# Two halves of a weight matrix loaded from two queues at the start of a decode-attention kernel

## The chip, the cores and the metric

The kernel runs on one core of one Trainium2 chip. The metric is device time in microseconds (us) of one launch; the time given for a kernel is the median of its runs. The engines are called as in the profile: PE (TensorE matmul, with PEld for its weight loads), DVE (VectorE), ACT (ScalarE), POOL (GpSimd), SP (SyncE, which here only issues DMAs; SPq and ACTq are the queues of issuing instructions). Matrices are bf16, sums are float32.

## What is computed

Two independent problems, A and B, with the same shapes and tensors of their own; the two outputs are put side by side. Each is one decode step of attention over the last 4096 rows of a cache of 16384:

```python
def _A_ref(x, k_cache, v_cache, wq, wo):        # x [2, 1, 576], caches [2, 16, 16384, 128]
    W = min(4096, max(256, Sk // 4))            # 4096
    rep = Hq // Hkv                             # 32 query heads, 16 key heads: 2
    q = (x @ wq).reshape(B, Sq, Hq, Dh).transpose(0, 2, 1, 3)
    k = jnp.repeat(k_cache[:, :, Sk - W:, :], rep, axis=1)
    v = jnp.repeat(v_cache[:, :, Sk - W:, :], rep, axis=1)
    scores = jnp.einsum("bhqd,bhkd->bhqk", q, k) * (Dh ** -0.5)
    p = softmax(scores, axis=-1)
    o = jnp.einsum("bhqk,bhkd->bhqd", p, v)
    return o.transpose(0, 2, 1, 3).reshape(B, Sq, Hq * Dh) @ wo    # wo [4096, 576]
return jnp.concatenate([a, b], axis=-1)
```

Everything is read once: 2 x 2 x 32 MB of keys and values, 4.5 MB of wq and 4.5 MB of wo for each problem.

## The kernel before, in words

**Order by hand.** The kernel lists operations for each engine in the order in which that engine runs them (`S.add(engine, function, deps, tag)`), and turns the dependences into semaphore waits; waits that follow from others are left out. So the place of a call in the code is the place of its instructions in that engine's queue.

**Slabs.** Keys and values come in slabs of 4 MB (128 partitions x 32 KB), each for one group of heads: 8 K slabs and 8 V slabs for each problem, 16 steps in all (`ND`). They go through a ring of four buffers (`ring`, `NR` = 4) that the first 512 rows of each wq share: buffers 0 and 1 hold wq of A and of B, 2 and 3 the first two K slabs. The next slab of a buffer is issued by SP when its last reader is done (L241). The stream is Q A, Q B, K0, K1, V0, K2, V1 and so on; near the end K14, K15, V13, V14, V15, and V15 is cut in two pieces (L237). Slabs of wo are issued in between (L275), the last of them after V15 in one part of 576 KB and three small ones (L277, L262).

**The start.** wq has 576 rows: four chunks of 128 (`NFC`, in the ring slab) and 64 left over, the half rows, loaded on their own into `wqr` (L248). The half rows of A stand on even partitions and those of B on odd ones, 64 partitions each. SP issues A's half rows, A's slab (L250), x of B (L185), B's half rows, B's slab, K0 and K1; ACT's first instruction is the DMA of A's x. `x_sb` holds the four rows of x (two of A, two of B). DVE writes `x_dup` (L361), the last 64 columns of x interleaved for the two problems and zeroed by the mask `maskP` where the other problem's partitions lie. Five transposing products on PE (L355) turn x into columns, ACT copies them to `xT` with four repeats (L369): chunks 0 to 3 and chunk 4, the half rows.

**The queries.** `do_qpair` (from L396) runs four times, twice for each problem: for each chunk one weight load of `xT` and four products of 512 columns into four PSUM banks (first of each chunk L421, the others L170, a helper that reuses the loaded weights). ACT evacuates the banks (L435, L440), DVE transposes (L445), ACT keeps the result (L453). The first product of each problem waits for its slab and for both loads of half rows. The four banks alternate between two sets from one pair to the next.

**A step.** DVE transposes the K slab in four parts (L485), PE multiplies them with the queries (L510, L170), DVE takes the maximum (L520, L533), ACT the exponential (L555), DVE transposes the probabilities (L563), PE multiplies them with V (L601, V one step behind), ACT evacuates (L613), and after each pair of steps a chain of small operations ends in the product with wo (L756 and, for the last pair, L760).

**The end.** After the last K slab the remaining steps run out: V13, V14 and V15's first piece (24 products, L601); `do_redist(D_ // 2, 2)` with two idle products (L711 to L716: products of 512 columns that write a bank nobody reads); V15's second piece (8 products); `keep_on(2)`, a weight load and two more idle products (L727 to L733); then the last combination (L648), norm (L683, DVE) and projections (L760): eight products for the pair's first step and eight for its second, of which four wait for the first small load of wo, two for the second and two for the third. ACT and DVE copy the two halves of the output (L792, L793), ACT and SP store them (L801).

Of the kernel before, what the change touches and what calls it, by code (L numbers as in the profile page):

```python
# [6 lines left out]
BF16 = mybir.dt.bfloat16  # L7
# [52 lines left out]
def build_kernel(nc, probs, out, cfg=None):  # L60
# [28 lines left out]
    HH = HD // 2  # L89
    NXC = NFC + 1  # L90
    NOUT = wo0.shape[1]
# [15 lines left out]
    with es:  # L107
        sb = lambda name, shape, dt: es.enter_context(nc.sbuf_tensor(name, shape, dt))
        ring = sb("ring", [128, NR, SLABW], BF16)
        xt = sb("xt", [128, NKT, 2048], FP32)  # L110
        wqr = sb("wqr", [128, HD], BF16)
        wob = sb("wob", [128, 2, 8, NOUT], BF16)
        xT = sb("xT", [128, NXC, NPROB, 128], BF16)
        x_dup = sb("x_dup", [NPROB * Bb, DREM, NPROB], BF16)
        maskP = sb("maskP", [NPROB * Bb, NPROB], BF16)
        x_sb = sb("x_sb", [NPROB * Bb, D], BF16)
# [45 lines left out]
        wo_sem = [sem("wo%d" % r) for r in range(2)]  # L162
        x_sem = [sem("xload%d" % P) for P in range(NPROB)]
        wl_sem = [sem("wl%d" % n_) for n_ in range(len(HEADS))]
# [19 lines left out]
        def load_x(P, eng):  # L184
            return dma_op(eng, x_sem[P], 1, lambda e: e.dma_start(  # L185
                x_sb[P * Bb:(P + 1) * Bb, :], probs[P][0][:, 0, :]).then_inc(x_sem[P], 16), [], "xload%d" % P)
        x_dma = {0: load_x(0, "act")}

# [55 lines left out]
        def issue_wq(n, P):  # L244
            wqP = probs[P][3]
            r = n % NR
            deps = [reader[n - NR]] if n >= NR else []
            wq_dma[P] = dma_op("sp", wq_sem, 1, lambda e: e.dma_start(  # L248
                wqr[P::NPROB, :], wqP[NFC * 128:D, :]).then_inc(wq_sem, 16), [], "wqr%d" % P)
            slab_dma[n] = dma_op("sp", ring_sem[r], 1, lambda e: e.dma_start(  # L250
                ring[:, r, :], wqP[0:NFC * 128, :].rearrange("(p s) n -> p (s n)", s=NFC)).then_inc(ring_sem[r], 16), deps, "wq%d" % P)

            if P == 0:
                for P_ in range(1, NPROB):
                    x_dma[P_] = load_x(P_, "sp")
# [90 lines left out]
        def f_xT(e, bank):  # L346
            last = None
            bb = bank[:].bitcast(BF16)
            NB = NPROB * Bb
            for ch in range(NXC):  # L350
# [4 lines left out]
                last = e.transpose(bb[:, ch * NB:(ch + 1) * NB], src, ident_b[0:NB, 0:NB])  # L355
            return last
        issue_until(0)
        init_small()
        init["maskP"] = S.add("dve", lambda e: e.tensor_reduce(
            maskP[:], ident_b[0:NPROB * Bb, 0:NPROB * Bb].rearrange("d (p b) -> d p b", b=Bb), AX.X, ALU.max), [p_ident_b], "maskP")  # L360
        x_cd = S.add("dve", lambda e: e.tensor_tensor(  # L361
            x_dup[:], x_sb[:, NFC * 128:D].unsqueeze(2).broadcast_to([NPROB * Bb, DREM, NPROB]),
            maskP[:].unsqueeze(1).broadcast_to([NPROB * Bb, DREM, NPROB]), ALU.mult), [init["maskP"]] + list(x_dma.values()), "xdup")

        n_x, bank_x, op_xT = tb_job(f_xT, "xT", list(x_dma.values()) + [x_cd, p_ident_b])

        def f_xev(e):
            NB = NPROB * NXC
            return e.activation(  # L369
                xT[:].rearrange("c h p (a w) -> c (h p) a w", a=4)[:, :, :, 0:Bb],  # L370
                bank_x[:].bitcast(BF16)[:, 0:NB * Bb].rearrange("c (p b) -> c p b", b=Bb).unsqueeze(2).broadcast_to([128, NB, 4, Bb]),
                ACTF.Copy)
        op_xev = S.add("act", f_xev, [op_xT, p_zxT], "xev")
        tb_consumer[n_x] = op_xev

# [20 lines left out]
        def do_qpair(i):  # L396
            Gs = (2 * i, 2 * i + 1)
            P = Gs[0] // GPP
            nq = pos[("Q", P)]
            issue_until(pos[("Q", NPROB - 1)])  # L400
            banks = q_banks(i)
            order = [NFC] + list(range(NFC))
            if Gs[0] % GPP:
                order = order[::-1]
            todo_ = [(ch, b) for ch in order for b in range(4)]
            seen = {b: 0 for b in range(4)}
            prev = [q_free.get((i - 2, b)) for b in range(4)]
            ends = [max(n for n, (ch, b) in enumerate(todo_) if b // 2 == g) + 1 for g in range(2)]
            assert ends[1] == len(todo_)
            for g in range(2):  # L410
                def fn(e, part=todo_[(0, ends[0])[g]:ends[g]]):
                    last = None
                    for ch, b in part:
                        c0 = (b % 2) * HH + 512 * (Gs[b // 2] % GPP)
                        w_ = ring[:, nq % NR, ch * HD + c0:ch * HD + c0 + 512] if ch < NFC else wqr[:, c0:c0 + 512]
                        start, stop = seen[b] == 0, seen[b] == NFC
                        seen[b] += 1
                        if q_first[0] == (P, ch):
                            last = matmul_again(e, q_first[1], banks[b], w_, start, stop, False)
                        else:  # L420
                            last = q_first[1] = e.matmul(banks[b], xT[:, ch, P, :], w_, start=start, stop=stop)  # L421
                            q_first[0] = (P, ch)
                    return last
                op = S.add("pe", fn, [slab_dma[nq], op_xev] + list(wq_dma.values()) + prev, "q%d" % Gs[g])
                reader[nq] = op
                q_done[Gs[g]] = op
# [268 lines left out]
        def do_redist(G, idle=0):  # L695
# [14 lines left out]
            if idle:  # L710
                def f_idle(e):  # L711
# [13 lines left out]
        fin_ops = []  # L725

        def keep_on(n):  # L727
            def f(e):
                first = last = e.matmul(idle_out, ident_b[:, :], maskB[:, :], start=True, stop=True)
                for _ in range(n - 1):  # L730
                    last = matmul_again(e, first, idle_out, maskB[:, :], True, True)
                return last
            S.add("pe", f, [chain[(ND - 1, "exp")], init["maskB"]], "keep%d" % n)  # L733

# [3 lines left out]
        def do_proj(D_):  # L738
# [255 lines left out]
```

## Time and profile before

| quantity | value |
|---|---|
| median of 3 runs | 363.48 us (363.40 to 363.51) |
| profiled execution: device time / span of its records | 363.62 us / 362.3 us |
| PE / PEld / DVE / ACT / POOL busy | 62% / 16% / 56% / 19% / 10% of the span |
| bytes read | 153.10 MB, 423 GB/s over the span |
| first load issued / first data packet | 0.80 us / 2.15 us |
| last wo load seen landed by PE / span ends | 360.2 us / 362.3 us |

Times in the profile count from the start of the span. A line of the timeline gives start and duration in us, the engine, the line of the kernel, the operation, the tile written and the tiles read, and in brackets how long the engine had been idle and for whom it waited. The DMA share of a stretch is the mean busy share of the core's 16 DMA engines; it can pass 1.00 a little, as a packet is counted where it starts. PEclk is the TensorE clock that was granted, 1.00 being full speed.

### The profile page before, as it was taken

What the parts mean: (1) busy time and instruction counts of PE and PEld (TensorE: products, weight loads), DVE (VectorE), ACT (ScalarE), POOL (GpSimd) and SP (SyncE); (2) the same over time, 40 slices, a digit from 0 to 9 for tenths busy, and PEclk for the clock granted to TensorE, in tenths of its full rate; (3) what the DMA queues carried; (4) which work ended last, traced back from release to release, by engine and by line L of the source; (5) the groups of instructions that cost most, each with busy time, mean ns of one, the idle gap of its engine ahead of it and who ended that gap; (6) DMA issues with size and microseconds to landing.
All of it is one profiled execution on the core that took longest, in us unless ns stands there. A gap on an engine that the chain in (4) does not pass through costs nothing.

```text
span 362.3 us, 2755 instructions
## 1 busy us (share of the span) xinstructions
PE 224.9 (62%) x1325; PEld 57.4 (16%) x950; DVE 201.5 (56%) x175; ACT 68.7 (19%) x153; POOL 35.3 (10%) x55
## 2 busy tenths in 40 slices
PE   0399195474865647584774747575673738656775
PEld 0000021111221201111121112111121112211121
DVE  3013598483917467291936648092854839179831
ACT  1036402020300303020210203112020203002131
POOL 1000000004000040004000040001200040110020
PEclk9999589788796968889787889969697887969999
DMA  8999999999999999999999999999999999999996
GB/s 348 405 445 423 445 408 433 456 412 442 420 426 434 434 409 447 430 438 430 402 454 430 434 434 418 434 434 430 421 434 430 438 425 430 430 434 434 425 419 242
DMA packets 6943, 153.27 MB, mean 423 GB/s; under 512 B 778, under 2 KB 1300, under 8 KB 1428
## 3 DMA queue, kind: packets, MB, share of 16 engines
q1 hardware_dynamic: 6924, 153.10, 98.7%
q8 instruction: 9, 0.15, 0.2%
q14 instruction: 2, 0.02, 0.0%
q10 hardware_dynamic: 8, 0.00, 0.0%
HBM read 153.10 MB, written 0.00 MB: 423 GB/s over the span
## 4 chain that ended last, share of the span: by engine, by line
DMA 71%; DVE 14%; PE 13%; SPq 1%; issue 0%
DMA ring<-in_B_k_cache_dram 34%; DMA ring<-in_A_k_cache_dram 26%; DVE xt L485 13%; DMA wob<-in_B_wo_dram 8%; PE st L170 6%; DMA wqr<-in_B_wq_dram 4%; PE st L510 4%; PE st L421 1%; PE tb L170 1%; PE acc L170 1%; PE ot L170 1%; DVE nM L533 1%; PE tb L421 0%; PE tb L523 0%; SPq L237 0%
## 5 line engine op out<-in xcount | busy, mean ns | idle before, releaser
L485 DVE STREAM_TRANSPOSE xt<-ring 128x2048 f32<-128x2048 f32 x64 | 145.3, 2285 | 77.3 <-DMA ring<-in_B_k_cache_dram 40.1
L510 PE MATMUL st<-xt,zq 128*128 128x512 bf16 x256 | 115.8, 452 | 114.5 <-DVE xt L485 88.8
L170 PE MATMUL st<-xt,zq 128*128 128x512 bf16 x256 | 114.4, 447 | 0.0
L510 PEld LDWEIGHTS st<-xt,zq 128*128 128x128 bf16 x256 | 27.9, 109 | 210.0 <-DVE xt L485 104.1
L601 PE MATMUL acc<-ring,pC 128*32 128x512 bf16 x512 | 33.9, 381 | 2.6 <-DMA ring<-in_B_v_cache_dram 2.6
L538 ACT ACTIVATE nMrep<-nM 1x128 f32<-1x128 f32 x16 | 4.9, 308 | 142.9 <-DVE nM L533 142.9
L613 ACT ACTIVATE acc_sb<-acc 128x512 bf16<-128x512 f32 x16 | 9.5, 597 | 81.3 <-PE acc L601 81.3
L563 DVE STREAM_TRANSPOSE pC<-pR 128x1024 bf16<-128x1024 bf16 x16 | 19.5, 1216 | 3.6 <-ACT pR L555 2.1
L520 DVE TENSOR_REDUCE m<-st 128x1 f32<-128x1024 f32 x16 | 19.0, 1190 | 1.2 <-PE st L170 1.2
L620 POOL TENSOR_TENSOR acc_sb<-acc_sb,maskJ 128x1024 bf16<-128x1024 bf16 (+1 forms) x8 | 13.4, 1679 | 59.0 <-ACT acc_sb L613 59.0
L472 POOL TENSOR_TENSOR zq<-qk,maskA 128x128 bf16<-128x128 bf16 x16 | 6.3, 399 | 127.9 <-PE st L170 106.1
L555 ACT ACTIVATE pR<-st,bias_sb 128x1024 bf16<-128x1024 f32 x16 | 17.8, 1114 | 0.5
L445 DVE STREAM_TRANSPOSE qtr<-qrow 128x512 f32<-128x512 f32 x8 | 5.7, 712 | 20.8 <-ACT qrow L435 13.5
L387 ACT ACTIVATE st<-maskB 128x1024 f32<-128x1024 bf16 x16 | 16.5, 1032 | 1.6 <-POOL rsel L570 0.4
L756 PE MATMUL ot<-wob,Rsb 128*2 128x512 bf16 x56 | 15.7, 399 | 0.2 <-ACT Rsb L721 0.2
L601 PEld LDWEIGHTS acc<-ring,pC 128*32 128x32 bf16 x512 | 12.9, 95 | 16.1 <-DMA ring<-in_B_v_cache_dram 3.6
L570 POOL TENSOR_TENSOR rsel<-maskS,rsum 128x16 f32<-128x16 bf16 x8 | 1.7, 216 | 124.1 <-ACT pR L555 124.1
L170 PE MATMUL tb<-wob,Rsb 128*2 128x64 bf16 x56 | 11.1, 197 | 0.0
L355 PE MATMUL tb<-ident_b,x_sb 4*128 4x4 bf16 x4 | 0.3, 173 | 14.6 <-DVE x_dup L361 14.6
L775 DVE TENSOR_TENSOR o_rest<-o_rest,tb 2x64 f32<-2x64 f32 x3 | 0.6, 209 | 15.4 <-PE tb L170 15.4
L623 POOL TENSOR_TENSOR acc_sb<-acc_sb 128x512 bf16<-128x512 bf16 (+1 forms) x8 | 8.2, 1030 | 0.6
L533 DVE TENSOR_REDUCE nM<-tb 1x8 f32<-1x128 f32 x16 | 4.4, 272 | 6.2 <-PE tb L523 6.1
(88 smaller groups left out, 107.0 us busy)
## 6 DMA issues: line engine op xcount, KB each, us to landing
ring<-in_A_k_cache_dram SPq DMA_DIRECT2D x8, 4096.0 KB, 30.8
ring<-in_A_v_cache_dram SPq DMA_DIRECT2D x8, 4096.0 KB, 32.1
ring<-in_B_k_cache_dram SPq DMA_DIRECT2D x8, 4096.0 KB, 30.7
ring<-in_B_v_cache_dram SPq DMA_DIRECT2D x7, 4096.0 KB, 32.8
wob<-in_A_wo_dram SPq DMA_DIRECT2D x4, 1152.0 KB, 33.5
ring<-in_A_wq_dram SPq DMA_DIRECT2D x1, 4096.0 KB, 12.8
ring<-in_B_wq_dram SPq DMA_DIRECT2D x1, 4096.0 KB, 22.4
wob<-in_B_wo_dram SPq DMA_DIRECT2D x3, 1152.0 KB, 34.6
```

Source lines behind the costliest of these rows:

```text
L170: return e.add_instruction(mybir.InstMatmult(name=nc.get_next_instruction_name(), engine=i.engine, ins=[e.lower_ap(rhs), i.ins[1]], outs=[ ...
L387: chain[(s, "fill")] = S.add("act", lambda e: e.activation(ST[s % 2][:, :].rearrange("k (h j) -> k h j", h=2), maskB[:].unsqueeze(1).broad ...
L485: Xop[(s, u)] = S.add("dve", lambda e: e.transpose(xt[:, i % NKT, :].rearrange("k (j w) -> k j w", w=64), ring[:, n % NR, :].bitcast(FP32) ...
L510: first = last = e.matmul(bank, zq[:, p4, s % NZQ, w0:w0 + 128], mv, start=False, stop=stop, skip_group_check=True)
L520: chain[(s, "max")] = S.add("dve", lambda e: e.tensor_reduce(m1[:, 0:1], ST[s % 2][:, :], AX.X, ALU.max), d, "max%d" % s)
L555: chain[(s, "exp")] = S.add("act", lambda e: e.activation(pR[:, :], ST[s % 2][:, :], ACTF.Exp, bias=bias_sb[:, 0:1], scale=SCALE, accum_ou ...
L563: chain[(s, "pC")] = S.add("dve", lambda e: e.transpose(pC[:, s % NPT, :, :].rearrange("k j c -> k (j c)"), pR[:, :]), d, "pC%d" % s)
L601: last = e.matmul(ACC[32 * cb:32 * cb + 32, 0:512], pC[:, D_ % NPT, j0_:j0_ + 4, :].rearrange("k j c -> k (j c)"), ring[:, n % NR, j0_ * 1 ...
L613: acc_ev[D_] = S.add("act", lambda e: e.activation(acc_sb[:, D_ % 2, :], ACC[:, :], ACTF.Copy), d, "accev%d" % D_)
L620: t = S.add("pool", lambda e: e.tensor_tensor(v, v, maskJ[:].unsqueeze(1).unsqueeze(3).broadcast_to([128, l1 - l0, 4, 128]), ALU.mult), [a ...
L623: t = S.add("pool", lambda e: e.tensor_tensor(a_[:, :, 0:256], a_[:, :, 0:256], a_[:, :, 256:512], ALU.add), [t], "acca%d" % D_)
L756: first = e.matmul(OT[0:Bb, 0:NB0], l_, wob[:, pc, s_, 0:NB0], start=start and begin, stop=end, skip_group_check=True)
```

## The change

It has three parts.

- **Loads.** `wqr` gets a place for each problem, `[128, 2, 2048]`: each of the 64 half rows is cut in two, so that a problem's half rows lie on all 128 partitions with 2048 columns each. B's load is issued by ACT as its first instruction, while SP issues A's; both x loads go to SP, behind A's slab, on one semaphore.
- **x.** `x_dup` holds the last 64 columns of x twice, without a mask; the products that turn x write four repeats at once; ACT copies the four full chunks, and a new DVE product writes two chunks for the half rows, each zeroed by `maskP` on the partitions of the other half (`xT` has six chunks). A query bank uses the one of these two chunks that its columns belong to, so each bank still gets five products. The second half of a pair of queries also waits for the evacuations of the pair before.
- **Tail.** Three idle products instead of two behind the redistribution, listed as waiting for `fin_ops` also; `keep_on` and its two idle products are gone; the first half of the last projection is in two parts, three quarters at once and the last quarter behind the last norm.

```diff
-        wqr = sb("wqr", [128, HD], BF16)
+        wqr = sb("wqr", [128, NPROB, HH], BF16)
...
-        x_dma = {0: load_x(0, "act")}
+        x_dma = {}
...
-            wq_dma[P] = dma_op("sp", wq_sem, 1, lambda e: e.dma_start(
-                wqr[P::NPROB, :], wqP[NFC * 128:D, :]).then_inc(wq_sem, 16), [], "wqr%d" % P)
+            if P == 0:
+                for P_ in (1, 0):
+                    wq_dma[P_] = dma_op("act" if P_ else "sp", wq_sem, 1, lambda e, P_=P_: e.dma_start(
+                        wqr[:, P_, :], probs[P_][3][NFC * 128:D, :].rearrange("r (h n) -> r h n", h=2)).then_inc(wq_sem, 16), [], "wqr%d" % P_)
...
             if P == 0:
-                for P_ in range(1, NPROB):
+                for P_ in range(NPROB):
                     x_dma[P_] = load_x(P_, "sp")
...
-                last = e.transpose(bb[:, ch * NB:(ch + 1) * NB], src, ident_b[0:NB, 0:NB])
+                last = e.matmul(bank[:, ch * 4 * NB:(ch + 1) * 4 * NB], src, ident_b[0:NB, 0:NB].rearrange(
+                    "k (p b) -> k p b", b=Bb).unsqueeze(2).broadcast_to([NB, NPROB, 4, Bb]), start=True, stop=True)
...
+        x_cd = S.add("dve", lambda e: e.tensor_copy(
+            x_dup[:], x_sb[:, NFC * 128:D].unsqueeze(2).broadcast_to([NPROB * Bb, DREM, 2])), list(x_dma.values()), "xdup")
         init["maskP"] = S.add("dve", lambda e: e.tensor_reduce(
-            maskP[:], ident_b[0:NPROB * Bb, 0:NPROB * Bb].rearrange("d (p b) -> d p b", b=Bb), AX.X, ALU.max), [p_ident_b], "maskP")
-        x_cd = S.add("dve", lambda e: e.tensor_tensor(
-            x_dup[:], x_sb[:, NFC * 128:D].unsqueeze(2).broadcast_to([NPROB * Bb, DREM, NPROB]),
-            maskP[:].unsqueeze(1).broadcast_to([NPROB * Bb, DREM, NPROB]), ALU.mult), [init["maskP"]] + list(x_dma.values()), "xdup")
+            maskP[:], ident_b[:].rearrange("d (r t) -> d t r", t=2), AX.X, ALU.max), [p_ident_b], "maskP")
...
+        def f_xev2(e):
+            return e.tensor_tensor(
+                xT[:, NFC:NXC].rearrange("c h p (a w) -> c h (p a) w", a=4)[:, :, :, 0:Bb],
+                bank_x[:, NFC * NB_:(NFC + 1) * NB_].rearrange("c (q b) -> c q b", b=Bb).unsqueeze(1).broadcast_to([128, 2, NPROB * 4, Bb]),
+                maskP[:].unsqueeze(2).unsqueeze(3).broadcast_to([128, 2, NPROB * 4, Bb]), ALU.mult)
+        op_xev = S.add("dve", f_xev2, [op_xev, op_xT, init["maskP"]], "xev2")
...
-            order = [NFC] + list(range(NFC))
+            mine = lambda ch: [b for b in range(4) if ch < NFC or b % 2 == ch - NFC]
+            order = [NFC, NFC + 1] + list(range(NFC))
...
-                op = S.add("pe", fn, [slab_dma[nq], op_xev] + list(wq_dma.values()) + prev, "q%d" % Gs[g])
+                before = [q_free.get((i - 1, b)) for b in range(4)] if g else []
+                op = S.add("pe", fn, [slab_dma[nq], op_xev] + list(wq_dma.values()) + prev + before, "q%d" % Gs[g])
...
-                S.add("pe", f_idle, [chain[(ND - 1, "exp")], init["maskB"]], "idle%d" % G)
+                S.add("pe", f_idle, [chain[(ND - 1, "exp")], init["maskB"]] + fin_ops, "idle%d" % G)
...
-                parts = [([(Rsb[:, pc, :, s_], s_) for s_ in range(4)], [r_ev[G], wo_dma[G]] + fin_ops, False, False, False)]
+                parts = [([(Rsb[:, pc, :, s_], s_) for s_ in ss], [r_ev[G], wo_dma[G]] + fin_ops + more, False, False, False)
+                         for ss, more in ((range(3), []), (range(3, 4), [norm[ND - 1]]))]
...
-        do_redist(D_ // 2, 2)
+        do_redist(D_ // 2, 3)
         do_PV(D_, range(PIECES[1][0] // JR, PIECES[1][1] // JR), pieces[1])
-        keep_on(2)
```

More of the change, by code (lines that the diff above doesn't have):

```diff
@@ L89, in build_kernel @@
     HH = HD // 2
-    NXC = NFC + 1
+    NXC = NFC + 2
     NOUT = wo0.shape[1]
@@ L110, in build_kernel @@
         xt = sb("xt", [128, NKT, 2048], FP32)
-        wqr = sb("wqr", [128, HD], BF16)
+        wqr = sb("wqr", [128, NPROB, HH], BF16)
         wob = sb("wob", [128, 2, 8, NOUT], BF16)
         xT = sb("xT", [128, NXC, NPROB, 128], BF16)
-        x_dup = sb("x_dup", [NPROB * Bb, DREM, NPROB], BF16)
-        maskP = sb("maskP", [NPROB * Bb, NPROB], BF16)
+        maskP = sb("maskP", [128, 2], BF16)
+        x_dup = sb("x_dup", [NPROB * Bb, DREM, 2], BF16)
         x_sb = sb("x_sb", [NPROB * Bb, D], BF16)
@@ L162, in build_kernel @@
         wo_sem = [sem("wo%d" % r) for r in range(2)]
-        x_sem = [sem("xload%d" % P) for P in range(NPROB)]
+        x_sem = sem("xload")
         wl_sem = [sem("wl%d" % n_) for n_ in range(len(HEADS))]
@@ L184, in load_x @@
         def load_x(P, eng):
-            return dma_op(eng, x_sem[P], 1, lambda e: e.dma_start(
-                x_sb[P * Bb:(P + 1) * Bb, :], probs[P][0][:, 0, :]).then_inc(x_sem[P], 16), [], "xload%d" % P)
-        x_dma = {0: load_x(0, "act")}
+            return dma_op(eng, x_sem, 1, lambda e: e.dma_start(
+                x_sb[P * Bb:(P + 1) * Bb, :], probs[P][0][:, 0, :]).then_inc(x_sem, 16), [], "xload%d" % P)
+        x_dma = {}
         p_ones_b = S.add("pool", lambda e: e.memset(ones_b[:], 1.0), [], "ones_b")
@@ L347, in f_xT @@
             last = None
-            bb = bank[:].bitcast(BF16)
             NB = NPROB * Bb
-            for ch in range(NXC):
+            for ch in range(NFC + 1):
                 if ch < NFC:
@@ L358, in build_kernel @@
         init_small()
+        x_cd = S.add("dve", lambda e: e.tensor_copy(
+            x_dup[:], x_sb[:, NFC * 128:D].unsqueeze(2).broadcast_to([NPROB * Bb, DREM, 2])), list(x_dma.values()), "xdup")
         init["maskP"] = S.add("dve", lambda e: e.tensor_reduce(
-            maskP[:], ident_b[0:NPROB * Bb, 0:NPROB * Bb].rearrange("d (p b) -> d p b", b=Bb), AX.X, ALU.max), [p_ident_b], "maskP")
-        x_cd = S.add("dve", lambda e: e.tensor_tensor(
-            x_dup[:], x_sb[:, NFC * 128:D].unsqueeze(2).broadcast_to([NPROB * Bb, DREM, NPROB]),
-            maskP[:].unsqueeze(1).broadcast_to([NPROB * Bb, DREM, NPROB]), ALU.mult), [init["maskP"]] + list(x_dma.values()), "xdup")
+            maskP[:], ident_b[:].rearrange("d (r t) -> d t r", t=2), AX.X, ALU.max), [p_ident_b], "maskP")
         n_x, bank_x, op_xT = tb_job(f_xT, "xT", list(x_dma.values()) + [x_cd, p_ident_b])
         def f_xev(e):
-            NB = NPROB * NXC
+            NB = NPROB * NFC * 4
             return e.activation(
-                xT[:].rearrange("c h p (a w) -> c (h p) a w", a=4)[:, :, :, 0:Bb],
-                bank_x[:].bitcast(BF16)[:, 0:NB * Bb].rearrange("c (p b) -> c p b", b=Bb).unsqueeze(2).broadcast_to([128, NB, 4, Bb]),
+                xT[:, 0:NFC].rearrange("c h p (a w) -> c (h p a) w", a=4)[:, :, 0:Bb],
+                bank_x[:, 0:NB * Bb].rearrange("c (q b) -> c q b", b=Bb),
                 ACTF.Copy)
         op_xev = S.add("act", f_xev, [op_xT, p_zxT], "xev")
+        NB_ = NPROB * 4 * Bb
+        def f_xev2(e):
[4 more added lines that the diff above has]
+        op_xev = S.add("dve", f_xev2, [op_xev, op_xT, init["maskP"]], "xev2")
         tb_consumer[n_x] = op_xev
@@ L401, in do_qpair @@
             banks = q_banks(i)
-            order = [NFC] + list(range(NFC))
+            mine = lambda ch: [b for b in range(4) if ch < NFC or b % 2 == ch - NFC]
+            order = [NFC, NFC + 1] + list(range(NFC))
             if Gs[0] % GPP:
                 order = order[::-1]
-            todo_ = [(ch, b) for ch in order for b in range(4)]
+            todo_ = [(ch, b) for ch in order for b in mine(ch)]
             seen = {b: 0 for b in range(4)}
@@ L414, in fn @@
                         c0 = (b % 2) * HH + 512 * (Gs[b // 2] % GPP)
-                        w_ = ring[:, nq % NR, ch * HD + c0:ch * HD + c0 + 512] if ch < NFC else wqr[:, c0:c0 + 512]
+                        w_ = ring[:, nq % NR, ch * HD + c0:ch * HD + c0 + 512] if ch < NFC else wqr[:, P, c0 - (b % 2) * HH:c0 - (b % 2) * HH + 512]
                         start, stop = seen[b] == 0, seen[b] == NFC
@@ L725, in build_kernel @@
         fin_ops = []
[L727 to L733, printed above, removed]
         def fin(half):
```

## The prediction

> **What bounds the kernel now.** I read the chain of waits first, then the slices of the span, then stages of my own cut. On the page of the kernel before, the slices, the DMA queues and the chain's shares by engine:
>
> ```profile
> DMA  8999999999999999999999999999999999999996
> GB/s 348 405 445 423 445 408 433 456 412 442 420 426 434 434 409 447 430 438 430 402 454 430 434 434 418 434 434 430 421 434 430 438 425 430 430 434 434 425 419 242
> ...
> q1 hardware_dynamic: 6924, 153.10, 98.7%
> ...
> DMA 71%; DVE 14%; PE 13%; SPq 1%; issue 0%
> ```
>
> The 16 DMA engines are busy from the first slice to the last, and 71% of the chain is DMA. The other 27% (DVE, PE) is how the inferred chain walks through issues; whether the DMA queue ever ran empty is read from the stages (columns: window, length, busy time and count of each engine, TensorE clock, DMA share, GB/s):
>
> ```profile
> 0.00:2.00 2.00, 0.00 (x0) 0.00 (x0) 0.92 (x2) 0.61 (x1) 0.70 (x6) 1.00 0.00 1
> 2.00:5.00 3.00, 0.00 (x0) 0.00 (x0) 1.89 (x10) 0.67 (x1) 0.29 (x1) 1.00 1.03 382
> 5.00:14.00 9.00, 0.00 (x0) 0.00 (x0) 0.00 (x0) 0.00 (x0) 0.00 (x0) 1.00 0.99 421
> ...
> 35.00:340.00 305.00, 190.79 (x1087) 50.44 (x784) 187.18 (x142) 53.74 (x112) 31.19 (x42) 0.84 1.00 431
> ...
> 358.00:360.20 2.20, 1.94 (x20) 0.65 (x19) 0.17 (x1) 0.60 (x1) 0.00 (x0) 1.00 0.47 163
> ```
>
> From 35 to 340 us the share is 1.00 at 431 GB/s: no compute delay reaches the transfers there. So the time is three pieces: 2.15 us until the first data packet, 357.7 us of transfers, and 2.5 us from the last landing to the end of the span. The change can move the first ramp and the tail; the bytes stay (153.10 MB).
>
> **The change, part by part.** The first instructions that matter, from the timeline:
>
> ```profile
> 0.80 0.56 SPq L248 DMA_DIRECT2D wqr<-in_A_wq_dram  x1
> 0.81 0.54 ACTq L185 DMA_DIRECT2D x_sb<-in_A_x_dram  x1
> ...
> 14.22 0.28 DVE L361 TENSOR_TENSOR x_dup<-x_sb,maskP 4x128 bf16<-4x128 bf16 x1 [10.33 <-DMA x_sb<-in_B_x_dram]
> ...
> 14.91 0.24 ACT L369 ACTIVATE xT<-tb 128x80 bf16<-128x80 bf16 x1 [12.24 <-PE tb L355]
> ...
> 15.70 0.58 PE L421 MATMUL st<-wqr,xT 128*128 128x512 bf16 x1 [0.82 <-DMA wqr<-in_B_wq_dram]
> ```
>
> *The loads.* B's half rows (512 KB) leave SP's third place, behind A's 4 MB slab, for ScalarE's first instruction, beside A's. The x of A takes the opposite way, to SP behind that slab. SP's queue becomes: A's half rows, A's slab, x A, x B, B's slab, two K slabs; before, its first six loads and x B were out by 4.8 us and none waited; the length stays seven. The table load behind ScalarE's DMA starts at 1.39 either way (both DMAs are one instruction; x A held the slot 0.54 us, the half-row loads 0.48 and 0.56). Bytes are unchanged. Half rows on 128 partitions are 128 packets of 4 KB in place of 64 of 8 KB, for each problem. The trace's DMA packets: 8 KB takes 0.309 us, 4.5 KB 0.181, 32 KB 1.213, so a 4 KB packet should take about 0.16 (estimate by the first two). Per DMA engine that is 16 x 0.16 = 2.56 against 8 x 0.309 = 2.47 us: **+0.09 us**.
>
> *The ramp* is not shown for two loaded queues, so it is bounded. From below: 2 to 5 us carried 382 against 431 GB/s, which loses 3 x 49/431 = 0.34 us, and 5 to 14 us loses 9 x 10/431 = 0.21 us; if a second queue filled all of that, **-0.55**. The first 16 packets took 0.5 to 0.8 instead of 0.309, which is where this loss sits. From above: x A, 2 rows, had its first packet 0.92 us after its issue, A's half rows, 64 rows, 1.35; by rows 128 would start 0.43 x 64/62 = 0.44 later, and a second queue that pays the 0.34 ramp again adds to **+0.8**. I take **0.0**, since the nearest row, B's half rows in the middle of a full queue, ran at 0.309 a packet, and two queues sharing an engine show no loss: a 16 KB instruction fetch among 32 KB packets made the longest of these 1.764 us, and 0.61 + 1.21 is 1.82.
>
> The Trainium skill, "DMA: Bandwidth & Descriptors", section "Issuing engines are not separate DMA queues", says that transfers started by different engines run on the same 16 DMA engines and interleave, and only the issuer's own time is saved. By it the ramp term is at most 0; the record of the shared fetch agrees.
>
> *The first products.* The x pair now lands behind 1 MB of half rows and A's slab rather than 0.5 MB: 0.524 MB / 433 GB/s = 1.2 us later, so 15.4 in place of 14.22. From there: doubling copy 0.28 and hand-over to 15.8; five transposing products, as before, to 16.1; ScalarE's copy 0.24 and then a new VectorE product with the mask, which waits for it, 0.25 by the 0.24 row of a small product from PSUM (L665): first q product at about 16.7, not 15.70. **+1.0 us on PE**, plus four more weight loads of 0.10. On DVE the new masks stand behind the wait for x; what they feed (fills) comes at 33 us. The new waits of the second half of a q pair for the evacuations of the pair before cost at most 0.3 (the last product starts at 35.08, and the evacuation with which that wait would end runs 34.35 to 35.35); behind it stand only K2's issue and PE's first scores. All of it is hidden: V0 is issued at 26.86 and K2 at 35.49 while the 17.8 MB issued at the start (17.8 / 0.431 = 41 us) last to about 43, and DVE, which falls behind here, has caught up by the third K slab:
>
> ```profile
> 68.34 2.31 DVE L485 STREAM_TRANSPOSE xt<-ring 128x2048 f32<-128x2048 f32 x1 [6.00 <-DMA ring<-in_A_k_cache_dram]
> ```
>
> It stood 6.00 us waiting for data. A start 1.3 us late leaves 4.7. **0 on the end**; if that cover were gone, at most +1.3.
>
> *The tail.* From the timeline:
>
> ```profile
> 357.37 0.61 PE L601 MATMUL acc<-ring,pC 128*32 128x512 bf16 x8 [0.42 <-DMA ring<-in_B_v_cache_dram]
> 357.92 0.39 PE L729 MATMUL st<-maskB,ident_b 128*128 128x512 bf16 x1
> ...
> 360.25 0.08 PEld L760 LDWEIGHTS st<-wob,oTn 128*2 128x2 bf16 x2 [0.28 <-DMA wob<-in_B_wo_dram]
> ...
> 360.58 0.45 DVE L793 CAST out_sb<-st 2x288 bf16<-2x288 f32 x1 [1.43 <-PE st L760]
> ```
>
> PE's last products wait for the last rows of wo, not for PE: they start at 360.25, when the load lands, after 0.28 us without work. The third idle product takes one more step of 0.22 (two products at 357.92 and 358.14 are that far apart); PE had 0.42 us free before 357.37, so **0**. The two products that go stood between the last value products and the wait for ScalarE's copy (to 358.64): **0**. The last quarter of the previous pair's projection now waits for the last norm: DVE has that at 359.15, while the six products ahead of it run to about 359.4, so **0**, and the waits that leave the next instruction only help products that start at 359.60, ahead of the landing. Sum: 0.09 + 0.0 + 0 + 0 = **+0.1 us**, against the 363.62 us of the profiled execution (span 362.3). That is 0.14 above the median 363.48, so on the median's scale 363.5 to 363.6; I say 363.5.
>
> **The rivals.** *A: the two queues fill the ramp.* For it: the first packets are slow, and a second queue brings work to the same engines. Against: those engines were already handed packets, four deep. Price -0.55 + 0.09: 363.0. It stays within 0.2%. To pass the 0.73 us that 0.2% is, the first byte would have to come earlier as well.
>
> *B: both starts are later.* 128 rows take the queue longer to hand out, twice. Price up to +0.8 + 0.09: 364.3, just beyond 0.2%.
>
> *C: PE loses its clock in the tail* (slower). The granted clock falls to 0.50 after a stretch in which PE did little:
>
> ```profile
> 34.10:37.50 3.40, 1.36 (x7) 1.00 1.07 463
> 37.50:40.90 3.40, 0.00 (x0) 0.50 1.07 463
> ...
> 78.50:81.90 3.40, 1.48 (x8) 1.00 0.97 417
> 351.50:354.90 3.40, 1.54 (x18) 1.00 0.91 383
> ```
>
> With 1.36 us of PE work in 3.4 us (and 1.42 from 139.9) the next stretch has half the clock; with 1.48 and 1.54 it keeps it. So it decides at about 1.45, and the stretch that holds PE's idle time from 352.99 to 354.88 is only 0.1 us above. The products that go come after that; without them the stretch from 354.9 still holds 2.90 - 0.45 + 0.22 = 2.7 us, far from the limit. Only if the first piece of V lands 0.1 us later beside PE does it fall. Then 24 value products, redistribution, three idle products and 8 more value products (1.48 + 0.20 + 0.65 + 0.61 = 2.9 us from 354.88) run at half speed: they end at 360.8 instead of 357.98 (+2.8), or at 359.6 (+1.6) if the next stretch from 358.4 is whole again. I take +2.0: 365.5. Against it: data and PE's work hang on the same landings and move together.
>
> The Trainium skill, "TensorE: Matmul & The Clock Gate", section "Why this matters for your kernels", warns of idle gaps of PE over some 3 us, a rule that speaks against taking the two products out. The drop at 37.5, after 2.06 us without a product, shows that a shorter gap suffices here; with the products out, the gap is 358.0 to 358.7.
>
> *D: the change does nothing at all to the time,* because every moved thing is under DMA. That is my forecast with its ramp at zero.
>
> **How the numbers follow.** Forecast (with D) 0.78: 363.5, its own range 363.2 to 363.9. A 0.10: 363.0, of which 0.05 beyond 0.2% for a first byte that comes sooner. B 0.06, half beyond. C 0.06. The range takes in the bounds of the ramp, -0.55 and +0.8: 362.9 to 364.3, and leaves out C and the parts beyond 0.2%, about 0.14. About 0.2% is what a measurement of this kernel can tell from no change. Faster by over 0.2% 0.05; within 0.2% 0.86; slower 0.09.
>
> **What would show it.** Right: half rows and slab A in flight by 2.2 us, 2 to 5 us at about 380 GB/s, first q product near 16.7, the wait ahead of the third K slab at 4 to 6 us, 431 GB/s in the middle, PE waiting for the last wo load and the clock at 1.00 from 354.9 on. Wrong: first data later than 2.5 us (B); 2 to 5 us above 420 GB/s (A); a clock of 0.50 behind 351 us (C); K slabs found landed by DVE, or a share below 0.97 in the middle, which I have excluded.

## The result, and the profile after

The changed kernel takes **364.88 us** (364.41 to 365.10, 6 runs) against 363.50 (363.37 to 363.58, 6 runs): ratio 1.0035, 95% interval 1.0023 to 1.0047. It is slower by 1.38 us; the prediction was 363.5 with a range of 362.9 to 364.3. The profiled execution took 364.93 us, its span 363.6.

On the page of the changed kernel, the slices, two queues and the chain's shares look as before:

```profile
DMA  8999999999999999999999999999999999999994
...
q1 hardware_dynamic: 6912, 152.58, 97.9%
...
q8 instruction: 9, 0.15, 0.2%
...
DMA 71%; DVE 16%; PE 8%; ACT 3%; SPq 1%; issue 1%
```

Only the last slice has fallen, from 6 to 4. The row q8 is the one to remember: nine packets of program, 0.2% of the DMA time. The stages (same columns as before):

```profile
0.00:2.00 2.00, 0.00 (x0) 0.00 (x0) 0.89 (x2) 0.77 (x1) 0.70 (x6) 1.00 0.16 27
2.00:5.00 3.00, 0.00 (x0) 0.00 (x0) 1.98 (x9) 0.52 (x1) 0.29 (x1) 1.00 1.07 400
5.00:14.00 9.00, 0.00 (x0) 0.00 (x0) 0.00 (x0) 0.00 (x0) 0.00 (x0) 1.00 1.02 440
...
35.00:340.00 305.00, 193.32 (x1089) 50.83 (x785) 187.19 (x142) 54.22 (x112) 31.22 (x42) 0.84 1.00 431
...
358.00:360.20 2.20, 0.84 (x12) 0.43 (x12) 0.17 (x1) 0.32 (x1) 0.00 (x0) 1.00 0.38 125
360.20:362.30 2.10, 0.95 (x8) 0.25 (x8) 0.45 (x1) 0.40 (x1) 0.00 (x0) 0.91 0.03 9
```

The start is a little faster (2 to 5 us: 400 GB/s, before 382), the middle unchanged at 431. The loss is in the last two rows: 125 GB/s where there were 163, and a rest of 0.03 after 360.2, where nothing was left before:

```profile
360.20:362.30 2.10, 0.29 (x2) 0.08 (x2) 0.45 (x1) 0.40 (x1) 0.00 (x0) 0.88 0.00 1
```

A share of 0.03 is half of one engine in sixteen, which fits one DMA engine that is still at work for a part of this stretch. The start and the third K slab, from the timeline of the changed kernel:

```profile
15.31 0.21 DVE L361 COPY x_dup<-x_sb 4x128 bf16<-4x128 bf16 x1 [11.33 <-DMA x_sb<-in_B_x_dram]
...
16.49 0.58 PE L431 MATMUL st<-wqr,xT 128*128 128x512 bf16 x1 [0.59 <-issue]
...
68.24 2.31 DVE L496 STREAM_TRANSPOSE xt<-ring 128x2048 f32<-128x2048 f32 x1 [5.54 <-DMA ring<-in_A_k_cache_dram]
```

These are as predicted: 15.31 (forecast 15.4), 16.49 (16.7), and a wait of 5.54 us ahead of the third K slab (4 to 6). The tail after, and the last products before:

```profile
357.05 0.62 PE L612 MATMUL acc<-ring,pC 128*32 128x512 bf16 x8 [0.20 <-DMA ring<-in_B_v_cache_dram]
358.37 0.26 PE L659 MATMUL tb<-ident_r,acc_sb 128*128 128x8 bf16 x4 [0.70 <-ACT acc_sb L624]
358.56 0.66 PE L764 MATMUL st<-wob,Rsb 128*2 128x288 bf16 x8
360.75 1.03 PE L764 MATMUL st<-wob,oTn 128*2 128x288 bf16 x8 [1.53 <-DMA wob<-in_B_wo_dram]
...
361.81 0.45 DVE L797 CAST out_sb<-st 2x288 bf16<-2x288 f32 x1 [2.98 <-PE st L764]
```

```profile
359.60 0.94 PE L760 MATMUL st<-wob,oTn 128*2 128x288 bf16 x8
```

V's second piece is there 0.32 us earlier than before (357.05, before 357.37), and yet the last products begin at 360.75 instead of 359.60, behind 1.53 us of waiting for the small wo loads. Between these two landings 1.5 us are lost ((360.75 - 357.05) - (359.60 - 357.37)), with PE's clock at 1.00 from 358.3 to 361.7.

**The packet records** say where. They hold 16 packets of 4 bytes for each large load, written as its data end; they are read here as one mark for each DMA engine. Before, the last marks come at 359.70, 359.72, 359.73 and 359.83. After, all but three are written by 359.43, and the last three stand 0.38 us apart at 360.26, 360.64 and 361.02: the three small loads on one engine. The last mark has moved by 1.19 us. PE's ninth 16 KB piece of program was read at 359.73 before, among the last data; after, at 358.17. It took 1.08 us. Behind it come 28 packets of 1152 bytes one after the other, as on one engine: the first six take 0.12 to 0.15 us each where others took 0.05, the rest 0.05 again, to 361.02. So that engine lost 1.08 + 0.49 = 1.57 us, and it ends 1.59 us behind the other fifteen.

### The profile page after: what moved, and what is told of

It is laid out like the page before. It is cut to its first block, busy times and chain, and to the rows that moved or that the text cites. A ratio compares the mean times of both kernels' runs of the same rounds, so it can differ in the third digit from the quotient of the medians.

```text
span 363.6 us, 2757 instructions
## 1 busy us (share of the span) xinstructions
PE 226.4 (62%) x1326; PEld 58.0 (16%) x953; DVE 201.7 (55%) x176; ACT 68.7 (19%) x153; POOL 35.3 (10%) x55
## 4 chain that ended last, share of the span: by engine, by line
DMA 71%; DVE 16%; PE 8%; ACT 3%; SPq 1%; issue 1%
DMA ring<-in_B_k_cache_dram 34%; DMA ring<-in_A_k_cache_dram 26%; DVE xt L496 14%; DMA wob<-in_B_wo_dram 8%; PE st L170 4%; DMA x_sb<-in_B_x_dram 4%; PE st L521 3%; ACT qrow L446 1%; DVE qtr L456 1%; ACT qk L464 1%; PE st L431 1%; ACT qrow L451 1%; DVE nM L544 1%; PE tb L534 0%; SPq L237 0%
## 5 line engine op out<-in xcount | busy, mean ns | idle before, releaser
L612 PE MATMUL acc<-ring,pC 128*32 128x512 bf16 x512 | 34.9, 390 | 2.2 <-DMA ring<-in_B_v_cache_dram 2.2
L612 PEld LDWEIGHTS acc<-ring,pC 128*32 128x32 bf16 x512 | 13.1, 97 | 16.7 <-DMA ring<-in_B_v_cache_dram 3.4
L560 ACT ACTIVATE bias_sb<-tb 128x1 f32<-128x1 f32 x16 | 2.7, 172 | 26.9 <-PE tb L554 26.9
```

Source lines behind the costliest of these rows:

```text
L612: last = e.matmul(ACC[32 * cb:32 * cb + 32, 0:512], pC[:, D_ % NPT, j0_:j0_ + 4, :].rearrange("k j c -> k (j c)"), ring[:, n % NR, j0_ * 1 ...
```

## The experiments

The first theory (F) was that this early fetch costs the time and that the split of the last projection lets it go early (without the split, PE's queue holds a separate wait for the first small wo load). Rivals: the new loads or ScalarE's queue leave one engine behind for the whole run (L); the missing idle products slow PE (P).

**Which half of the change.** `s1_start_alone` has the new start and the old tail, `s2_tail_alone` the old start and the new tail.

Against the changed kernel, s1 is (s2 puts the opposite edits into the kernel before):

```diff
-                S.add("pe", f_idle, [chain[(ND - 1, "exp")], init["maskB"]] + fin_ops, "idle%d" % G)
+                S.add("pe", f_idle, [chain[(ND - 1, "exp")], init["maskB"]], "idle%d" % G)
...
-                parts = [([(Rsb[:, pc, :, s_], s_) for s_ in ss], [r_ev[G], wo_dma[G]] + fin_ops + more, False, False, False)
-                         for ss, more in ((range(3), []), (range(3, 4), [norm[ND - 1]]))]
+                parts = [([(Rsb[:, pc, :, s_], s_) for s_ in range(4)], [r_ev[G], wo_dma[G]] + fin_ops, False, False, False)]
...
-        do_redist(D_ // 2, 3)
+        do_redist(D_ // 2, 2)
         do_PV(D_, range(PIECES[1][0] // JR, PIECES[1][1] // JR), pieces[1])
+        keep_on(2)
```

> The new start with the old tail (two idle products, two more behind the last value products, the projection in one part). Theory F: the loss is PE's last 16 KB instruction fetch, which came at 359.73 us before and comes at 358.17 in the changed kernel, between the last wo packets, because the separate wait for the first small wo load, which held PE's sequencer back, is gone with the tail's edits. The old tail brings that wait back: fetch at about 359.4, the start's lead of 0.3 us stays, 363.2 us. Theory L (the new start leaves one DMA engine behind the others until the end): 364.9. Theory P (the idle products taken out cost the time): 363.2 or 363.5.

> The old start with the new tail. Theory F: the separate wait is gone, the fetch falls at about 358.4 between the last wo packets, one DMA engine ends 1.5 us behind the others: 364.9 to 365.2 us. Theory L: 363.5, as before the change. Theory P: 364.9 or more.

Measured: s1 364.93 us, 1.0038 [1.0026, 1.0051], fetch at 358.36, one engine's last mark at 361.02. s2 363.55, 0.9997 [0.9988, 1.0006], fetch at 359.73, last mark 359.72. The start alone carries the loss, though it gains at the start. The first theory is in trouble, since s1 has no split.

**The split by itself.** `s3_one_part` takes it out of the changed kernel (the edit of `parts` above and nothing else); `s4_two_parts` puts it alone into the kernel before (the same edit the other way):

```diff
-                parts = [([(Rsb[:, pc, :, s_], s_) for s_ in range(4)], [r_ev[G], wo_dma[G]] + fin_ops, False, False, False)]
+                parts = [([(Rsb[:, pc, :, s_], s_) for s_ in ss], [r_ev[G], wo_dma[G]] + fin_ops + more, False, False, False)
+                         for ss, more in ((range(3), []), (range(3, 4), [norm[ND - 1]]))]
```

> The changed kernel with the last projection's first half in one part again, so that the next instruction waits both for the norm and for the first small wo load, the latter as a separate wait; still three idle products and no others. Theory F: fetch at about 359.4, 363.2 us. Theory L: 364.9. Theory P: 364.9, since the idle products stay out.

> The kernel before with one edit, the last projection's first half in two parts, which removes the separate wait for the first small wo load; all idle products stay. Theory F: the fetch comes early, 364.9 to 365.2 us. Theory L: 363.5. Theory P: 363.5.

Measured: s3 364.88, 1.0037 [1.0023, 1.0050], fetch at 358.77, last mark 360.94; s4 363.47, 0.9998 [0.9989, 1.0007], fetch at 359.53. The split decides nothing, and the first theory's second half falls. Its first half stands: the longer time and the early fetch go together in all six profiles.

**Idle products of the tail.** Two theories are left. F2: the fetch still costs the time, and PE's place in its program moves it. Q: the loads from ScalarE's queue let it in early or leave an engine behind. The changed kernel with two (`a_two_idle`), and in the same line with none (`a_no_idle`):

```diff
-        do_redist(D_ // 2, 3)
+        do_redist(D_ // 2, 2)
```

> The changed kernel with two idle products in place of three, one PE instruction less; all loads as changed. Theory F2: the wait stands at 2226, the fetch starts about 359.4, the start's lead of 0.3 us is kept: 363.2 us. Theory Q: 364.9.

> The changed kernel with no idle product at all. Theory F2: the wait stands at 2224, the fetch starts about 359.4; 363.2 us, if PE keeps its clock without the idle products (2.1 us of PE work in the 3.4 us from 355 on). Theory Q: 364.9. If the idle products are needed for the clock, some 0.5 us or more on top of either.

Measured: a_two_idle 364.81, 1.0032 [1.0020, 1.0044], fetch at 358.31, last mark 360.77. a_no_idle 363.45, 0.9996 [0.9987, 1.0005], fetch at 359.37, last mark 359.47. With two idle products the time is that of theory Q, with none it is near that of theory F2. So fewer idle products are not what costs, and the new loads don't leave an engine behind: a_no_idle has all of them. Three products that do nothing cost 1.4 us by standing in the program.

**A few PE instructions at the start.** To the kernel before, two or three instructions are added (a weight load and one or two products that nobody reads), at 1.43 us, when PE waits for x; `a_hundred_more` adds 100 to the changed kernel. Shown is `b_three_more`; `range(0)` makes it `b2_two_more`, `range(98)` the other.

```diff
+        def f_pad(e):
+            first = last = e.matmul(ST[1][:, 0:128], ident_b[:, :], ones_b[:, :], start=True, stop=True)
+            for _ in range(1):
+                last = matmul_again(e, first, ST[1][:, 0:128], ones_b[:, :], True, True, False)
+            return last
+        S.add("pe", f_pad, [p_ident_b], "pad")
```

> The kernel before with two PE instructions more at the start (a weight load and a product into a bank that the queries overwrite), long before any data. Two theories are left after the first four runs, in which the start alone gave 364.93 us, the tail alone 363.55. Theory F2: the loss is the fetch between the last wo packets as before, but what moves it is PE's place in its program, not a wait: the 16 KB block is asked for when PE passes one certain instruction. In the three kernels with the old start the wait for the last value copy stands at instruction 2224 to 2226, and the fetch starts 1.0 us behind that wait; with the new start it stands at 2227 to 2229, and the fetch comes 0.3 us behind to 0.2 us ahead of its end. So the instruction lies at 2226 or 2227, and two more at the start put it ahead of the wait: fetch at about 358.5, 364.9 to 365.2 us. Theory Q: it is the loads from ScalarE's queue that let the fetch in early, or leave an engine behind; with the old start 363.5.

> The changed kernel with 100 PE instructions more at the start, so that the block is asked for 100 instructions earlier, before the first piece of V15, and falls among packets of 24 KB or 8 KB instead of 1152 B. Theory F2: it then costs one engine the 0.6 us of its own transfer or less: 363.2 to 363.9 us. Theory Q: 364.9, as no load is changed.

Measured: b2_two_more 363.61, 1.0007 [0.9997, 1.0017], fetch at 360.10. a_hundred_more 365.62, 1.0067 [1.0047, 1.0086], fetch at 352.25, and V's first piece landed for PE at 356.10 instead of 354.56. Both expectations of theory F2 failed: two more instructions were to do what three then did, and the hundred were to cost less, not more. The ten profiles have one order by the compiled programs: what counts is the place of the product that waits for V's second piece, not the later wait that theory F2 took. (The place is that of its weight load, counted from 0 with all weight loads, products and separate waits.) It is 2207 before. The new start puts three instructions ahead of it (four more weight loads, one separate wait less), the third idle product a fourth: 2211. In every profile with 2210 or more the fetch is early, with 2209 or less late. The likely working: the request goes out as PE's queue passes instruction 2209, either before that wait or behind it. That was put to the test with one product more than in b2_two_more:

> The kernel before with one weight load and two idle products added to PE's program after the identity is made (3 PE instructions more, at a time when PE is idle; the loads, the queues and the tail are untouched). Theory G: PE's ninth 16 KB piece of program is asked for when PE's queue passes one fixed place of its program, instruction 2209 counted with weight loads; what decides is whether that instruction stands ahead of the product that waits for the second piece of V (that product is instruction 2207 before, 2209 with two more, 2211 after). In all ten profiles so far the fetch came at 358.2 to 358.8 (352.3 with a hundred more) where that product was 2210 or later, and at 359.4 to 360.1 where it was 2209 or earlier. Here it is 2210, so: fetch at 358.2 to 358.9, one DMA engine ending at 360.9 to 361.1 while the others end by 359.9, and 364.6 to 365.0 us, 1.0030 to 1.0042 of before. Rival L, the loss comes from the new loads or ScalarE's queue: old loads here, so 363.5, ratio 1.000, fetch at 359.5 or later, no late engine.

Measured: **364.86 us, 1.0034 [1.0021, 1.0047]**, fetch at 358.13, last mark 360.89. Old loads, old queues, old tail, and the whole loss, from a single idle product more, at 1.5 us, than in b2_two_more. The tails of PE in b2_two_more and in b_three_more:

```profile
359.62 0.93 PE L766 MATMUL st<-wob,oTn 128*2 128x288 bf16 x8
```

```profile
360.71 0.93 PE L766 MATMUL st<-wob,oTn 128*2 128x288 bf16 x8 [1.52 <-DMA wob<-in_B_wo_dram]
...
361.68 0.45 DVE L799 CAST out_sb<-st 2x288 bf16<-2x288 f32 x1 [2.88 <-PE st L766]
```

The same eight products begin 1.09 us later, behind a wait of 1.52 for the small wo loads.

**The same boundary from the other side.** `a_one_and_two` is the changed kernel with one idle product ahead of that wait and two behind it (place 2209). `a_one_two_sp` gives B's half rows back to SP and A's x to ScalarE, keeping their new layout.

```diff
-        do_redist(D_ // 2, 3)
+        do_redist(D_ // 2, 1)
         do_PV(D_, range(PIECES[1][0] // JR, PIECES[1][1] // JR), pieces[1])
+        keep_on(2)
```

In a_one_two_sp, besides:

```diff
-        x_dma = {}
+        x_dma = {0: load_x(0, "act")}
...
-            if P == 0:
-                for P_ in (1, 0):
-                    wq_dma[P_] = dma_op("act" if P_ else "sp", wq_sem, 1, lambda e, P_=P_: e.dma_start(
-                        wqr[:, P_, :], probs[P_][3][NFC * 128:D, :].rearrange("r (h n) -> r h n", h=2)).then_inc(wq_sem, 16), [], "wqr%d" % P_)
+            wq_dma[P] = dma_op("sp", wq_sem, 1, lambda e: e.dma_start(
+                wqr[:, P, :], wqP[NFC * 128:D, :].rearrange("r (h n) -> r h n", h=2)).then_inc(wq_sem, 16), [], "wqr%d" % P)
...
-                for P_ in range(NPROB):
+                for P_ in range(1, NPROB):
```

> The changed kernel with one idle product ahead of the product that waits for the second piece of V and a weight load with two idle products behind that piece's products, in place of three ahead. Against the kernel with two idle products (364.8 us) one product less stands ahead of that wait, so it is instruction 2209 and not 2210. Theory G: the fetch comes at 359.3 to 360.1, no engine is late, the clock stays whole, the start's lead of 0.3 us is kept to the end: 363.1 to 363.3, ratio 0.9990 to 0.9995, span 361.9 to 362.1. Rival L: the new start makes one engine late whatever the tail: 364.8, one engine ends at 361.0. Rival I, the idle products decide by their number (three in all, as in the changed kernel): 364.8 too, with the fetch at 358.2.

> The kernel a_one_and_two with the half rows of B issued by SyncE again, behind A's slab and B's x, and A's x by ScalarE as its first instruction (the order of the queues before); the half rows stay in the new layout on 128 partitions and the rest of the new start stays. It parts the start's lead of 0.3 us. If the lead comes from ScalarE's issue of the half rows, beside SyncE's: first data at 2.1 to 2.2 us, the wait for K slabs ends as before (68.34, 110.20, 276.76, 318.40), 363.4 to 363.6. If it comes from the layout (smaller packets fill the engines sooner): the waits end 0.3 earlier, 363.1 to 363.3. In both the fetch comes at 359.3 or later and no engine is late.

Measured: a_one_and_two 363.47, 0.9995 [0.9986, 1.0003], fetch at 359.62; a_one_two_sp 363.21, 0.9991 [0.9982, 1.0000], fetch at 359.31. Neither has a late engine. In the timeline of a_one_and_two PE's last products follow the eight ahead of them without a break, with no wait of 0.4 us or more for a small load, and the output copy starts 1.3 us sooner than in the changed kernel:

```profile
359.38 1.08 PE L772 MATMUL st<-wob,oTn 128*2 128x288 bf16 x8
...
360.50 0.45 DVE L805 CAST out_sb<-st 2x288 bf16<-2x288 f32 x1 [1.49 <-PE st L772]
```

Both beat the changed kernel; neither is shown to beat the one before, though a_one_two_sp is at the edge of it. Its lead, if real, doesn't come from ScalarE's queue: with SP alone issuing, its half rows have their first packet at 1.84 us, before the change 2.15.

**Is it a place, or the ninth fetch?** By the place alone, a whole period of 256 instructions more must bring the same case back. The changed kernel gets 253 or 256 idle instructions at the start (as above, products of 32 columns, `range(251)` and `range(254)`), which brings the place to 2464 = 2208 + 256 and to 2467 = 2211 + 256. They end at 8.2 us, before x lands.

> The changed kernel with 253 more PE instructions (a weight load and 252 products of 32 columns) while PE waits for x; the rest is untouched, its tail with three idle products too. Theory G with a period of 256 instructions (the gaps between fetches in all profiles): the product that waits for the second piece of V is instruction 2464 here, and 2464 less 256 is 2208, below the 2210 from which the fetch came early. So a tenth fetch stands at 359.3 or later, no engine is late at the end, and the changed kernel gets faster by 253 idle instructions: 363.2 to 363.7, ratio 0.999 to 1.0005. At worst the one more fetch of 16 KB at the start costs its engine some 0.6 us that stays: 364.0. Rival M, any PE instruction more makes it slower (2 more 363.6, 3 more 364.9, 100 more 365.6): 365 or more. If the 253 products last beyond 16.5 us, the first product of the queries moves by as much, which the wait of 4 to 5 us ahead of the K slabs hides.

> The kernel a_253_more with three more of the same idle products at the start, 256 in all. Theory G: the product that waits for the second piece of V is instruction 2467, 2211 after one period is taken off, as in the changed kernel: the fetch is back at 358.1 to 358.8, one engine ends at 360.8 to 361.1, and 364.6 to 365.0 us. Rival M: as a_253_more, within 0.1.

Measured: a_253_more 364.74, 1.0029 [1.0018, 1.0039]; a_256_more 364.92, 1.0036 [1.0023, 1.0050]. **Both are slower than before; the expectation failed for the first.** Its tenth fetch came at 359.59, late enough, but this doesn't show that the place works with a period of 256. PE got V's first piece at 356.00, not 354.56, and the fetch stands 3.59 us behind that, like the early fetch of the changed kernel (3.61); in the seven kernels with a late fetch it is 4.8 to 5.2. One engine was behind already when V's first piece landed. The page and the timeline of a_253_more:

```profile
q8 instruction: 10, 0.16, 0.2%
```

```profile
356.00 1.48 PE L618 MATMUL acc<-ring,pC 128*32 128x512 bf16 x24 [1.88 <-DMA ring<-in_B_v_cache_dram]
```

Why it was behind is found in the marks of the big slabs. Each row is one slab: time of its first mark, then the 16 marks as us behind it, in order.

```
changed kernel (fetches at 61.36 100.45 138.67 177.21 212.80 253.26 294.73 340.17 358.17)
 55.98: 0.0 0.1 0.1 0.2 0.2 0.3 0.3 0.4 0.4 0.4 0.4 0.5 0.5 0.5 0.5 0.8     none late
 65.70: 0.0 0.1 0.1 0.2 0.2 0.3 0.3 0.3 0.4 0.4 0.4 0.5 0.5 0.5 0.8 2.1     1 late
149.01: 0.0 0.1 0.2 0.2 0.3 0.3 0.3 0.4 0.4 0.5 0.7 0.8 1.1 1.9 2.0 2.0     3
232.33: 0.0 0.1 0.1 0.1 0.3 0.3 0.4 0.5 0.7 0.8 1.0 1.8 1.8 1.9 2.0 2.0     5
315.61: 0.0 0.0 0.1 0.3 0.4 0.5 0.7 0.8 1.0 1.7 1.8 1.8 1.8 1.9 2.0 2.0     7
344.75: 0.0 0.0 0.1 0.4 0.5 0.7 0.8 1.0 1.7 1.8 1.8 1.8 1.8 1.9 1.9 2.0     8
a_253_more (fetches at 8.85 62.44 100.69 138.81 178.89 219.30 253.60 294.80 343.01 359.59)
335.17: 0.0 0.1 0.3 0.4 0.5 0.5 0.8 0.9 1.6 1.7 1.8 1.9 2.0 2.1 2.1 2.1     8
344.88: 0.0 0.0 0.3 0.4 0.5 0.5 0.8 0.9 1.6 1.7 1.9 2.0 2.1 2.1 2.1 3.3     8, one twice
```

Each fetch puts one engine back by about 1.55 us: between the rows ahead of it and behind it one mark leaves its place and comes in that much later (0.3 in the row of 315.61 is 1.8 in that of 344.75; with two digits, 1.54 to 1.56 for each of the first eight in the changed kernel). It stays back, as all 16 engines are full until the end. Eight fetches put back eight different engines, so from the first to the eighth the last landing moves only once. **The ninth goes to an engine that is already late** (1.8 becomes 3.3), and the end moves by another 1.2. In a_256_more the row at 344.89 ends in 3.1, likewise. (Its 364.92 us lie in the expected range, but not for the expected reason. Its tenth fetch came at 359.33, not at 358.1 to 358.8: in this profile PE also had half its clock from 349.49 to 356.32 and reached V's second piece at 358.58.) In all fifteen profiles the first eight fetches leave eight late engines. In all eight slower ones the ninth comes 2 us or more before the last mark, and one engine ends 1.2 to 1.6 us behind the other fifteen; in all seven others the ninth comes at 359.3 or later, at most 0.11 us before the last mark.

| kernel | place of the wait | ninth fetch, us | last mark, us | median, us | ratio |
|---|---|---|---|---|---|
| before | 2207 | 359.73 | 359.83 | 363.50 | 1 |
| s4_two_parts | 2207 | 359.53 | 359.64 | 363.47 | 0.9998 |
| s2_tail_alone | 2208 | 359.73 | 359.72 | 363.55 | 0.9997 |
| a_no_idle | 2208 | 359.37 | 359.47 | 363.45 | 0.9996 |
| b2_two_more | 2209 | 360.10 | 359.82 | 363.61 | 1.0007 |
| a_one_and_two | 2209 | 359.62 | 359.62 | 363.47 | 0.9995 |
| a_one_two_sp | 2209 | 359.31 | 359.36 | 363.21 | 0.9991 |
| s1_start_alone | 2210 | 358.36 | 361.02 | 364.93 | 1.0038 |
| b_three_more | 2210 | 358.13 | 360.89 | 364.86 | 1.0034 |
| a_two_idle | 2210 | 358.31 | 360.77 | 364.81 | 1.0032 |
| changed kernel | 2211 | 358.17 | 361.02 | 364.88 | 1.0035 |
| s3_one_part | 2211 | 358.77 | 360.94 | 364.88 | 1.0037 |
| a_hundred_more | 2311 | 352.25 | 361.03 | 365.62 | 1.0067 |
| a_253_more | 2464 | 343.01 | 360.91 | 364.74 | 1.0029 |
| a_256_more | 2467 | 340.41 | 360.73 | 364.92 | 1.0036 |

a_hundred_more costs 0.75 us beyond the others that are slower. There V's first piece is what the late engine brings late (356.10), PE works 1.00 us in that stretch, and the clock is halved in the next, as rival C of the prediction had it:

```profile
353.42:356.83 3.41, 1.00 (x19) 0.41 (x20) 0.61 (x2) 0.36 (x1) 0.00 (x0) 1.00 0.92 375
356.83:360.20 3.37, 3.37 (x29) 0.48 (x18) 0.00 (x0) 0.18 (x1) 0.00 (x0) 0.50 0.60 221
```

The Trainium skill, "Runtime: NRT & Kernel Launch", section "Instruction fetch mechanics", says that an engine's program is refilled in blocks of 16 KiB, 256 instructions, and that crossing a boundary costs one DMA tail-bump, mostly hidden. The traces agree on the blocks: the packets have 16384 bytes, and with 256 instructions more there is one fetch more, at 9.90 us, and the next eight come within 1.3 us of the changed kernel's first eight. They do not agree on the cost, and the measurement decides: about 1.55 us of one DMA engine each, and 1.25 us of the kernel for the ninth (364.86 against 363.61).

**What stays open.** That the request leaves at instruction 2209 is worked out from the places above, not recorded; that the place comes back after 256 instructions is not shown, as PE was late in both kernels that were to test it. Which engine serves a fetch isn't recorded either; that the ninth returns to one of the first eight is seen in the marks, and why it does is not shown.

## Why the prediction was wrong

- **What bounds the kernel: right.** DMA is full from 35 to 340 us at 431 GB/s in both, and PE waits for the last rows of wo.
- **The loads, the ramp and 4 KB packets, +0.1: right within what can be measured.** 2 to 5 us carried 400 GB/s (forecast about 380), so some of rival A is there. The half rows' first packet comes at 1.82 to 1.92 us in the ten kernels with the new layout and at 2.15 to 2.17 in the five with the old one, so more rows did not make it later, as the upper bound of the ramp assumed. But one profile's lead of 0.3 us at the K slabs is less than it looks: the last K slab lands at 318.08 to 318.43 in five profiles with the old start (mean 318.30) and at 317.95 to 318.33 in ten with the new one (mean 318.14). With the ninth fetch late, the new start gives 0.9995 and 0.9996. The rule of the Trainium skill that was weighed there, "DMA: Bandwidth & Descriptors", section "Issuing engines are not separate DMA queues", is borne out: with the issue back on SP, a_one_two_sp is not slower (0.9991).
- **The first products: right** in time (16.49) and in their cover (a wait of 5.54 us).
- **The tail by itself: right.** The new tail on the old start gives 0.9997, the split alone 0.9998. Rival C did not come about in the changed kernel.
- **The step that failed** is the sum of the terms that were put at nothing for PE: "plus four more weight loads of 0.10", "the third idle product takes one more step of 0.22 [...] so **0**" and, over both, "PE's last products wait for the last rows of wo, not for PE". Each was priced as time on an engine that has time to spare. PE does wait for wo, but the landing of wo itself hangs on how many instructions PE's program has ahead of one wait: three from the start and one from the tail bring the ninth fetch 1.56 us forward (359.73 to 358.17), onto an engine that was late, and the last mark of wo from 359.83 to 361.02. In the kernel before, two more instructions cost nothing and three cost all of it. The signs of being right that the prediction named for the middle and the tail all came (431 GB/s, PE waiting for wo, a whole clock); none of them was the time at which wo lands.
- A row of the profile before was misread: "a 16 KB instruction fetch among 32 KB packets made the longest of these 1.764 us" was taken to show that two queues share an engine without loss. That packet begins at 220.11, where the fetch of 219.11 ends after 1.02 us. The fetch's own time comes on top: 1.02 + (1.764 - 1.213) = 1.57 us, where 16 KB at the rate of the 32 KB packets would be 0.61. The page also had q8 with nine packets; the ninth, at 359.73, 0.1 us before the last mark, has no part in the prediction.
- None of the rivals had this cause. B came nearest in its number (364.3) but its first byte was to come later, and it came earlier (1.83 us, before 2.15); that the time came out near its price is chance.

## What to carry to other kernels

In a kernel that is bound by DMA to its end, instructions of an idle engine are not always free: its program comes through the same DMA engines. Look up when each fetch of program is served and which landings it holds back, count how far an edit moves the boundary against the next wait, and keep the last fetch behind the last load. A cheap test is to add a few instructions that do nothing at a place where the engine waits: here one such product more gave the whole loss without any of the change.

## What the runs showed of the hardware

- A 16 KB fetch of PE's program puts one DMA engine back by about 1.55 us for the rest of a saturated stream. In the stream it takes 0.95 to 1.11 us itself, and the 32 KB packet that starts as it ends takes 1.68 to 1.76 us, not 1.21. Eight fetches put back eight engines; a ninth that came before the last loads had ended, one of these again.
- The queue whose DMA is issued first is not always the one served first: with both half rows issued at 0.80 us, ScalarE's 5 or 6 ns ahead in all three, ScalarE's had the first packet in the changed kernel (1.83 us, SP's 2.46), SP's in a_one_and_two (1.83, ScalarE's 2.25) and in s1_start_alone (1.83 and 2.71).
- The limit of about 1.45 us of PE work in 3.4 us, below which the prediction saw the clock halved, is no safe one. In a_no_idle, PE worked 1.91 us of a stretch and had half the clock in the next:

```profile
356.22:359.63 3.41, 1.91 (x26) 0.72 (x26) 0.17 (x1) 0.74 (x2) 0.00 (x0) 1.00 0.74 272
359.63:362.00 2.37, 0.67 (x4) 0.08 (x2) 0.45 (x1) 0.40 (x1) 0.00 (x0) 0.50 0.00 1
```
